# Residual row loads on SyncE, and the softmax's second half one PV step earlier, in a two-layer attention and token-MLP kernel

## The chip, the cores and the metric

The kernel runs on one core of one Trainium2 chip. The metric is the device time of one execution in microseconds. Of the kernel before, five runs gave a median of 1326.21 us (1325.14 to 1326.72). A difference of under some 0.2% between two kernels can hardly be told from none.

A core has five engines, each of which works through its own instructions in order: TensorE (matmuls into PSUM banks; PE in the profile, with PEld for the weight loads), VectorE (DVE), ScalarE (ACT), GpSimd (POOL) and SyncE (SP), which only issues DMA transfers. DMA transfers are issued by SyncE, GpSimd and ScalarE and carried out by 16 DMA engines. In the profile, q1 holds the transfers of SyncE and q0 those of GpSimd.

## The reference

Two kinds of residual layer alternate, twice: `x = x + A(layernorm(x))`, then `x = x + B(layernorm(x))`. x is 2048 rows by 1024 columns in bf16.

```
def A(x):   # 32 heads of 32; each row sees itself and 7 rows before it, 2 rows apart
    q, k, v = split(x @ wqkv)
    idx = pos[:, None] - 2 * arange(8)
    logits = einsum("bhsd,bhswd->bhsw", q, k[idx]) * 32 ** -0.5   # -1e9 where idx < 0
    o = einsum("bhsw,bhswd->bhsd", softmax(logits), v[idx])
    return o @ wo

def B(x):   # an MLP over the row axis S, not over the columns
    u = gelu(einsum("bsd,sf->bdf", layernorm(x), w1) + b1)        # F = 3584
    return (einsum("bdf,fs->bds", u, w2) + b2).transpose
```

## The kernel before

Since the window steps by two, even and odd rows never meet in A. They are two classes, c = 0 and 1, of 1024 rows each, held as 8 tiles of 128 rows. One layer of the program (`li` = 0 or 1, called layer 1 and layer 2 below) is one A and one B.

**Attention** of a class goes through two groups of 512 columns, so a layer has four groups, n = 0 to 3 (0 and 1 are class 0). For each group, `qk` (L431 to L444) multiplies q by eight shifted copies of k on VectorE (L439) and lets TensorE sum over each head with a selection matrix (L444). The softmax over the eight offsets is in two halves. `softmax_front` (L448) copies the logits, masks them, subtracts the maximum (last L455) and takes exp on ScalarE (L456). `softmax_back` (L458) sums, takes the reciprocal and multiplies (L461 to L465), stores the probabilities Pb in DRAM (L468) and calls `spread` (L474), which loads them back with each head's row repeated over 32 partitions, in two loads of 1 MB, one for each half hf of the rows (L482). These tiles, pb, come from a pool of two buffers. `pv` (L484) is a generator of steps: for one group, half of its columns and one hf, it yields two steps, dq = 0 and 1. A step is two products (L500), two additions (L504) and one more that writes oT (L506), all on VectorE; its scratch tile shares two buffers with qk's.

`stream` (L509) sets the order: in the second half of group n, qk, `softmax_front(n)`, the projections of the next columns, the hf = 0 steps of `pv(n - 1, ...)`, `softmax_back(n)`, the hf = 1 steps. After the last group come the eight PV steps of group 3 with no qk ahead of them; in layer `li` = 1, `ahead` does the same for group 1 in the middle.

**Output projection.** `out_proj` (L590) multiplies oT by wo, adds the residual row tile xr (VectorE, L625 or L628), stores the sum xn in DRAM on GpSimd (L630) and normalises it for B. `fetch` (L605) loads xr two tiles ahead; the load is issued by GpSimd (L608).

**MLP.** `gemm1` (L645) applies w1; `gemm2_tile` (L670) applies w2 to one row tile: it loads the residual rows xs, issued by GpSimd (L672), runs 56 matmuls, 28 for each half of the columns into a PSUM bank of its own, evicts them with bias and residual (VectorE, L686) into xo, stores xo on GpSimd (L692), normalises it into hb and has SyncE transpose hb into hT for the next attention (L233).

**Buffers and queues.** The row tiles xr, xn, xs, xo, hb, the scratch tiles junk and tmp share one pool, x2, of four slots, handed out as they come free. The weight tiles wo, w1, w2 and some of wv share a pool of five, and are loaded on SyncE, as are the wq tiles and the transposes. So SyncE's queue carries weights and transposes; GpSimd's carries row loads, row stores, Pb and pb.

**Order of the work.** The program's order is made in two stages. `weave` counts estimated times of TensorE and VectorE from the yields and places units of "filler" (the second class's GEMM2, projections ahead of time, the output projection of class 0, partial sums of GEMM1) between the attention's units. Then the framework's scheduler goes through all instructions by priority (their place in the program), with a model of times and of free slots, and fixes the order on every engine and queue; each instruction then waits on semaphores for what it needs. A lower instruction can so move ahead of a higher one that isn't ready in the model.

Of the kernel before, what the change touches and what calls it, by code (L numbers as in the profile page):

```python
# [15 lines left out]
P = 128  # L16
# [10 lines left out]
def kernel(  # L27
# [13 lines left out]
    nc = tc.nc  # L41
# [139 lines left out]
    def rows(t):  # L181
        return t.rearrange("(i m) d -> i m d", m=P)
# [166 lines left out]
    class Attn:  # L349
# [131 lines left out]
                src = bass.AP(base.tensor, base.offset, [(4 * SB * W * TB, CH), (0, P // CH), (1, 4 * W * TB)])  # L481
                nc.gpsimd.dma_start(out=pb[:].rearrange("p b u t -> p (b u t)"), in_=src)  # L482

        def pv(self, n, half, hf):  # L484


            c = n // NCQ
            for dq in (2 * half, 2 * half + 1):
                dt = (n % NCQ) * DQ + dq
                if hf == 0 and c and dt < 2 * DIL:  # L490
                    self.oT[c][dt] = v_t[dt // 2][:, dt % 2, PADK + 8:PADK + 8 + SC]
                elif hf == 0:
                    self.oT[c][dt] = otp.tile([P, SC], BF16, name="oT", tag="oT")[:]
                waits = [("pb", n, hf)] + ([] if c else [("ready", 2, dt)])
                yield "dve", 4.7, waits, [("free", 2, dt % 2), "oT"] if hf else [], 0.0, 0.0
                pb = self.pbs[(n, hf)]
                pr = tpl.tile([P, 4, W, TB], BF16, name="pr", tag="T")
                for par in range(2):
                    u = slice(4 * par, 4 * par + 4)
                    nc.vector.tensor_tensor(out=pr[:, :, u, :], in0=pb[:, :, u, :],  # L500
                                            in1=window(self.v_of(c, dt), par, 2 + hf * HT, [(TB, 4), (2, 4), (1, TB)]),
                                            op=ALU.mult)
                for wd in (4, 2):
                    nc.vector.tensor_tensor(out=pr[:, :, 0:wd, :], in0=pr[:, :, 0:wd, :], in1=pr[:, :, wd:2 * wd, :],  # L504
                                            op=ALU.add)
                nc.vector.tensor_tensor(out=self.oT[c][dt][:, hf * HT:(hf + 1) * HT].rearrange("p (b t) -> p b t", t=TB),  # L506
                                        in0=pr[:, :, 0, :], in1=pr[:, :, 1, :], op=ALU.add)

        def stream(self, lead):  # L509


            last = DIL * NCQ - 1
            PC = KD // 2

            def where(n, half):
                return n // NCQ, (n % NCQ) * (DQ // 2) + half

            def qk_proj(n, half):
                c, pair = where(n, half)
                if c == 1 and pair == 0:  # L520
                    yield "drain", "second"
                yield from self.proj_pair(c, pair, (1, 0))

            def v_proj(n, half):
                if n < NCQ:
                    yield from self.proj_pair(*where(n, half), (2,))

            def opened_by(n):
                if n == NCQ - 1:
                    yield "open", "out0"  # L530
                    yield "open", "partials"
                elif n == NCQ:
                    yield "open", "late"

            def ahead():
                c, pair = where(NCQ - 1, 1)
                for half in range(self.early):
                    if half:
                        for dt in (2 * pair, 2 * pair + 1):
                            for hf in range(2):  # L540
                                yield from self.proj(c, 2, dt, hf)
                    for hf in range(2):
                        yield from self.pv(NCQ - 1, half, hf)
                if self.early == 2:
                    yield from opened_by(NCQ - 1)

            yield from lead if lead is not None else qk_proj(0, 0)
            yield "open", "second"
            if lead is not None:
                yield "drain", "second"  # L550
            yield "open", "v_ahead"
            for n in range(last + 1):
                done = self.early if n == NCQ else 0
                for half in range(2):
                    nx = (n + half, 1 - half)
                    turn = nx == (NCQ, 0) and self.li > 0
                    yield from self.qk(n, 2 * half)
                    yield from self.qk(n, 2 * half + 1)
                    if half:
                        yield from self.softmax_front()  # L560
                    if lead is not None and nx == (0, 1):
                        for u in ((0, 2, 1), (0, 3, 0), (0, 3, 1),):
                            yield from self.proj(0, *u)
                    elif nx[0] <= last and not turn:
                        yield from qk_proj(*nx)
                    if n - 1 == NCQ and half == 0:
                        yield "drain", "v_ahead"
                    pv = n > 0 and half >= done
                    if pv:
                        yield from self.pv(n - 1, half, 0)  # L570
                    if half:
                        yield from self.softmax_back(n)
                    if pv:
                        yield from self.pv(n - 1, half, 1)
                        if half:
                            yield from opened_by(n - 1)
                    if n > 0 and half == 0 and done < 2:
                        yield from v_proj(n - 1, 1)
                    if half:
                        yield from v_proj(n, 0)  # L580
                    if nx == (NCQ, 0):
                        yield from ahead()
                    if turn:
                        yield from qk_proj(*nx)
            yield "drain", "out0"
            for half in range(2):
                for hf in range(2):
                    yield from self.pv(last, half, hf)

    def out_proj(at_, c, res, dst, h2, on_act):  # L590

        if not on_act:
            yield "pe", 0.0, ["oT"], [], 0.0
        dst_v = rows(dst)
        wo_t = [[None, None] for _ in range(NDC)]
        for n in range(NDC):
            for hf in range(2):
                wt = wb("wo", [P, KD // 2, 512])
                nc.sync.dma_start(out=wt[:], in_=wo_v[hf, :, :, n * 512:(n + 1) * 512])
                wo_t[n][hf] = wt  # L600
        for hf in range(2):
            h2[c][hf] = hx(f"h2{c}{hf}", [P, NT // 2, D])
        xrs = []

        def fetch():  # L605
            if len(xrs) < NT:
                xrs.append(x2("xr"))
                nc.gpsimd.dma_start(out=xrs[-1][:], in_=res[len(xrs) - 1])  # L608

        fetch()  # L610
        fetch()
        for i in range(NT):
            if not on_act:
                yield "pe", 3.5, ["oT"], [], 3.6
            xr = xrs[i]
            xn = x2("xn")
            s1 = st("s1", [P, NDC]) if on_act else None
            for n in range(NDC):
                ps = bank()
                xs_ = slice(n * 512, (n + 1) * 512)  # L620
                for kt in range(KD):
                    nc.tensor.matmul(ps[:], lhsT=at_.oT[c][kt][:, i * P:(i + 1) * P], rhs=wo_t[n][kt // 4][:, kt % 4, :],  # L622
                                     start=(kt == 0), stop=(kt == KD - 1))
                if on_act:
                    nc.vector.scalar_tensor_tensor(out=xn[:, xs_], in0=ps[:], scalar=1.0, in1=xr[:, xs_], op0=ALU.mult,  # L625
                                                   op1=ALU.add, accum_out=s1[:, n:n + 1])
                else:
                    nc.vector.tensor_tensor(out=xn[:, xs_], in0=ps[:], in1=xr[:, xs_], op=ALU.add)  # L628
            fetch()
            nc.gpsimd.dma_start(out=dst_v[i], in_=xn[:])  # L630
            h = h2[c][i // 4][:, i % 4, :]
            if on_act:
                nm, rs = stats_act(xn[:], 1.0 + EPS, eps2, h, s1)
                norm_act(h, xn[:], nm, rs)
                yield 3.5, 0.0
            else:
                mean, rs = stats_dve(xn[:], 1.0 + EPS, eps2)
                norm_dve(h, xn[:], mean, rs)
# [30 lines left out]

    def gemm2_tile(c, i, w2t, src, dst, hT, on_act=False, end=False):  # L670
        xs = x2("xs")
        nc.gpsimd.dma_start(out=xs[:], in_=src[c][i * P:(i + 1) * P, :])  # L672
        xo = x2("xo")
        halves = [slice(n * 512, (n + 1) * 512) for n in range(NDC)]
        groups = [halves[:1], [slice(512, 768)], [slice(768, 1024)]] if end else [halves]
# [105 lines left out]
    for li in range(2):  # L781
# [3 lines left out]
        res = [xin_v[c] for c in range(DIL)] if first else [rows(xb[c]) for c in range(DIL)]  # L785
# [89 lines left out]
```

## Time and profile before

| | |
|---|---|
| median of 5 runs | 1326.21 us (1325.14 to 1326.72) |
| the profiled execution's own time | 1326.21 us |
| its span, first to last instruction | 1324.4 us |
| mean granted TensorE clock | 0.987 |
| VectorE, ScalarE, GpSimd busy | 52%, 33%, 7% |
| DMA | 173 MB, 131 GB/s on average |
| median us to landing: xs (256 KB), xr (256 KB, from the input), pb (1 MB) | 3.9, 3.9, 11.0 |
| median us to landing: w2 tile (448 KB), w1 tile (512 KB) on SyncE | 3.8, 4.4 |

The profile is one execution on the chip. A group of instructions is named by engine, line and tiles: `xo<-ps,b_sb,xs` writes xo and reads ps, b_sb and xs. Waits are listed as who waited for whom, with total time, number and longest. The stages of the span, with the busy time of TensorE and VectorE in each:

| stretch, us | work | TensorE busy | VectorE busy |
|---|---|---|---|
| 0 to 200 | layer 1: class 0 prepared, its attention | 186.8 of 200 | 167.5 |
| 200 to 341 | class 1's attention, output projections, partial GEMM1 | 133.0 of 141 | 122.4 |
| 341 to 478 | GEMM1 | 136.8 of 137 | 30.4 |
| 478 to 574 | GEMM2 of class 0 | 96.0 of 96 | 24.1 |
| 574 to 781 | GEMM2 of class 1, woven with layer 2's attention of class 0 | 198.6 of 207 | 136.2 |
| 781 to 972 | class 1's attention, output projections, partial GEMM1 | 182.4 of 191 | 146.3 |
| 972 to 1128 | GEMM1 | 156.0 of 156 | 33.2 |
| 1128 to 1324 | GEMM2 of both classes | 193.3 of 196 | 23.6 |

TensorE idles almost only in the stretches with attention.

### The profile page before, as it was taken

The page shows a single profiled execution, that of the slowest core. Times are in us where ns is not written, and L with a number is a line of the kernel's source. Part 1 is how long each engine was busy: PE and PEld are TensorE (multiplying, and loading weights), DVE is VectorE, ACT ScalarE, POOL GpSimd, SP SyncE. Part 2 cuts the span into 40 slices and gives each one's busy share as a digit, 9 for nine tenths or more (in the row PEclk, how much of TensorE's full clock was granted, in tenths as well). Part 3 has the DMA queues.
Part 4 walks back from the last instruction along what each step waited for, and adds up shares of the span by engine and source line. Part 5 has one row for each costly group of instructions (what it writes and reads, how often), then busy time and mean ns, then how long its engine had stood idle before and what let it go on. Part 6 is the DMA issues. An engine that isn't in the chain of part 4 may idle for free.

```text
span 1324.4 us, 15430 instructions
## 1 busy us (share of the span) xinstructions
PE 1282.9 (97%) x6284; PEld 576.8 (44%) x6284; DVE 683.5 (52%) x861; ACT 439.7 (33%) x740; POOL 95.5 (7%) x230
## 2 busy tenths in 40 slices
PE   9998998999999999999997999999899999999999
PEld 4343443443444444444443444444344444444444
DVE  6779997989202322234796734878950033111111
ACT  6844445731213420024434425475122234000000
POOL 3000001101000000000001010011010000000000
PEclk9998999998999999999998999999899999999999
DMA  9652535562522248864658762438162232334432
GB/s 259 156 119 65 134 98 147 162 159 86 144 84 76 76 137 215 217 171 117 159 151 231 195 177 64 96 113 230 49 198 64 74 86 72 118 96 137 118 117 61
DMA packets 239448, 173.00 MB, mean 131 GB/s; under 512 B 32208, under 2 KB 227152, under 8 KB 237328
## 3 DMA queue, kind: packets, MB, share of 16 engines
q1 hardware_dynamic: 224432, 116.67, 32.7%
q0 software_dynamic: 14368, 54.29, 14.9%
q8 instruction: 49, 0.80, 0.3%
q10 hardware_dynamic: 576, 1.05, 0.2%
q14 instruction: 23, 0.19, 0.1%
HBM read 146.81 MB, written 18.87 MB: 125 GB/s over the span
## 4 chain that ended last, share of the span: by engine, by line
PE 65%; DVE 12%; DMA 6%; issue 1%; ACT 1%; DVEq 0%; POOL 0%; POOLq 0%
PE ps L681 24%; PE ps L655 22%; PE ps L409 11%; PE ps L622 6%; DVE pr L500 5%; DVE pr L504 4%; DMA xs<-xa 2%; DMA xa<-xn 1%; DMA pb<-pd 1%; PE sc L444 1%; DMA wq<-in_A_wqkv_dram 1%; DMA pd<-Pb 1%; DVE xo L686 1%; DVE T L439 1%; DMA hT<-hb 0%
## 5 line engine op out<-in xcount | busy, mean ns | idle before, releaser
L681 PE MATMUL ps<-g,w 128*128 128x512 bf16 (+1 forms) x1820 | 391.1, 377 | 7.5 <-DVE xo L686 7.5
L655 PE MATMUL ps<-h,w 128*128 128x512 bf16 x1792 | 388.2, 379 | 1.9 <-ACT h L230 1.3
L681 PEld LDWEIGHTS <-w 128*128 128x128 bf16 x1820 | 177.8, 98 | 218.9 <-issue 12.2
L655 PEld LDWEIGHTS <-w 128*128 128x128 bf16 x1792 | 175.3, 98 | 214.1 <-issue 3.3
L409 PE MATMUL ps<-hT,wq 128*128 128x512 bf16 (+1 forms) x1112 | 243.7, 376 | 2.1 <-DMA hT<-hb 1.1
L686 DVE SCALAR_TENSOR_TENSOR xo<-ps,b_sb,xs 128x512 bf16<-128x512 f32 (+1 forms) x65 | 45.6, 738 | 254.9 <-PE ps L681 230.6
L666 DVE TENSOR_TENSOR tmp<-ps,g 128x512 f32<-128x512 f32 x80 | 55.3, 692 | 227.4 <-PE ps L655 227.4
L439 DVE TENSOR_TENSOR T<-q,k 128x4096 bf16<-128x4096 bf16 x60 | 136.0, 2287 | 65.7 <-ACT q L413 54.1
L409 PEld LDWEIGHTS <-wq 128*128 128x128 bf16 x1112 | 108.6, 100 | 132.5 <-issue 12.7
L504 DVE TENSOR_TENSOR pr<-pr 128x2048 bf16<-128x2048 bf16 (+1 forms) x128 | 119.3, 948 | 0.1
L622 PE MATMUL ps<-wo,oT 128*128 128x512 bf16 x384 | 93.8, 386 | 13.0 <-DVE oT L506 9.3
L409 PE MATMUL ps<-hT,wv 128*128 128x512 bf16 x448 | 104.6, 388 | 0.0
L416 ACT CAST k<-ps 128x1024 bf16<-128x1024 f32 x60 | 60.9, 1016 | 78.0 <-PE ps L409 78.0
L500 DVE TENSOR_TENSOR pr<-pb,v 128x2048 bf16<-128x2048 bf16 x64 | 75.9, 1215 | 17.9 <-DMA pb<-pd 14.3
L667 ACT ACTIVATE g<-tmp,b_sb 128x512 bf16<-128x512 f32 x80 | 57.7, 721 | 82.1 <-DVE tmp L666 82.1
L500 DVE TENSOR_TENSOR pr<-pb,g 128x2048 bf16<-128x2048 bf16 x64 | 76.3, 1216 | 10.9 <-DMA pb<-pd 10.9
L409 PEld LDWEIGHTS <-wv 128*128 128x128 bf16 x448 | 49.2, 113 | 53.0 <-issue 10.7
L661 ACT CAST g<-ps 128x512 bf16<-128x512 f32 x80 | 45.5, 591 | 68.7 <-PE ps L655 68.6
L192 ACT ACTIVATE ln<-mv,eps 128x1 f32<-128x1 f32 x37 | 10.9, 295 | 164.2 <-DVE mv L201 156.8
L622 PEld LDWEIGHTS <-oT 128*128 128x128 bf16 x384 | 37.3, 99 | 63.4 <-issue 11.7
L413 ACT CAST q<-ps 128x512 bf16<-128x512 f32 x60 | 35.0, 585 | 52.2 <-PE ps L409 52.2
L444 PE MATMUL sc<-T,sel 128*32 128x512 bf16 x512 | 39.3, 394 | 11.5 <-DVE T L439 11.4
(94 smaller groups left out, 632.8 us busy)
## 6 DMA issues: line engine op xcount, KB each, us to landing
w<-in_B_w_dram SPq DMA_DIRECT2D x96, 448.0 KB, 3.8
w<-in_B_w_dram SPq DMA_DIRECT2D x56, 512.0 KB, 4.4
wq<-in_A_wqkv_dram SPq DMA_DIRECT2D x38, 512.0 KB, 4.2
pb<-pd POOLq DMA_DIRECT2D x16, 1024.0 KB, 11.0
wo<-in_A_wo_dram SPq DMA_DIRECT2D x16, 512.0 KB, 4.4
xa<-xn POOLq DMA_DIRECT2D x32, 256.0 KB, 3.5
xs<-xa POOLq DMA_DIRECT2D x32, 256.0 KB, 3.9
wv<-in_A_wqkv_dram SPq DMA_DIRECT2D x14, 512.0 KB, 6.7
```

What stands on the lines that cost most here:

```text
L409: nc.tensor.matmul(ps[:, lo:hi], lhsT=cols, rhs=self.hT[c][hf][:, kt, lo:hi], start=(kt == 0), stop=(kt == KD - 1))
L416: nc.scalar.copy(out=window(buf, 0, PADK + hf * HT, [(KW + 1, 2), (1, HT)]), in_=ps[:].unsqueeze(1).to_broadcast([P, 2, HT]))
L439: nc.vector.tensor_tensor(out=T[:], in0=q.unsqueeze(1).to_broadcast([P, 4, SC]), in1=window(k, par, 2, [(2, 4), (1, SC)]), op=ALU.mult)
L444: nc.tensor.matmul(self.sc[32 * gr:32 * gr + 32, par], lhsT=sel[:, sb * DQ + dq, :], rhs=T[:, :, b * TB:(b + 1) * TB], start=(dq == 0 and ...
L500: nc.vector.tensor_tensor(out=pr[:, :, u, :], in0=pb[:, :, u, :], in1=window(self.v_of(c, dt), par, 2 + hf * HT, [(TB, 4), (2, 4), (1, TB) ...
L504: nc.vector.tensor_tensor(out=pr[:, :, 0:wd, :], in0=pr[:, :, 0:wd, :], in1=pr[:, :, wd:2 * wd, :], op=ALU.add)
L622: nc.tensor.matmul(ps[:], lhsT=at_.oT[c][kt][:, i * P:(i + 1) * P], rhs=wo_t[n][kt // 4][:, kt % 4, :], start=(kt == 0), stop=(kt == KD - 1))
L655: nc.tensor.matmul(ps[:], lhsT=wt[c][:, i, fl * P:(fl + 1) * P], rhs=h2[c][i // 4][:, i % 4, dc * 512:(dc + 1) * 512], start=(k == 0), sto ...
L666: nc.vector.tensor_tensor(out=tmp[:], in0=ps[:], in1=gs, op=ALU.add)
L667: nc.scalar.activation(out=gs, in_=tmp[:], func=ACT.Gelu_apprx_tanh, bias=b1_sb[:, ft:ft + 1])
L681: nc.tensor.matmul(ps[:, 0:xc.stop - xc.start], lhsT=w2t[n][:, ft % HF, c::DIL], rhs=g[ft // GF][:, ft % GF, xc], start=(ft == 0), stop=(f ...
L686: nc.vector.scalar_tensor_tensor(out=xo[:, xc], in0=ps[:, 0:xc.stop - xc.start], scalar=b2_sb[:, i, c:c + 1], in1=xs[:, xc], op0=ALU.add, ...
```

## The change

The change has two parts; the second and third points below belong together.

- The loads of the residual rows, xr in `out_proj` and xs in `gemm2_tile`, are issued by SyncE and not by GpSimd: 32 loads of each kind, 256 KB apiece. The stores of the rows stay on GpSimd.
- `pv` takes an argument `dqs`, the steps to make; by default both, as before.
- In `stream`, of the two hf = 0 steps of `pv(n - 1, ...)`, only dq = 0 stands ahead of `softmax_back(n)`; dq = 1 comes after it. In the half without a `softmax_back` the two steps follow each other as before. The oT tiles of the columns are handed out in the same order.

```diff
-        def pv(self, n, half, hf):
+        def pv(self, n, half, hf, dqs=(0, 1)):
 
 
             c = n // NCQ
-            for dq in (2 * half, 2 * half + 1):
+            for dq in (2 * half + x for x in dqs):
                 dt = (n % NCQ) * DQ + dq
@@ stream
                     pv = n > 0 and half >= done
                     if pv:
-                        yield from self.pv(n - 1, half, 0)
+                        yield from self.pv(n - 1, half, 0, (0,))
                     if half:
                         yield from self.softmax_back(n)
                     if pv:
+                        yield from self.pv(n - 1, half, 0, (1,))
                         yield from self.pv(n - 1, half, 1)
@@ out_proj
         def fetch():
             if len(xrs) < NT:
                 xrs.append(x2("xr"))
-                nc.gpsimd.dma_start(out=xrs[-1][:], in_=res[len(xrs) - 1])
+                nc.sync.dma_start(out=xrs[-1][:], in_=res[len(xrs) - 1])
@@ gemm2_tile
         xs = x2("xs")
-        nc.gpsimd.dma_start(out=xs[:], in_=src[c][i * P:(i + 1) * P, :])
+        nc.sync.dma_start(out=xs[:], in_=src[c][i * P:(i + 1) * P, :])
```

## The prediction

> **What bounds the kernel now.** I read the page first, then TensorE's waits, then the order of time around each of its stalls on every queue that the change touches.
>
> ```profile
> span 1324.4 us, 15430 instructions
> PE 1282.9 (97%) x6284; PEld 576.8 (44%) x6284; DVE 683.5 (52%) x861; ACT 439.7 (33%) x740; POOL 95.5 (7%) x230
> ```
>
> TensorE is the bound. Nothing here takes matmuls away, so the gain can only come from its 1324.4 - 1282.9 = 41.5 us of idle time and from matmuls that ran at half clock after a stall. The waits of TensorE over the run, longest first in total (us, times, longest):
>
> ```profile
> PE sc L444 <- DVE T L439: 11.4, 3, 5.3
> PE ps L622 <- DVE oT L506: 9.3, 3, 6.1
> PE ps L681 <- DVE xo L686: 7.5, 1, 7.5
> PE ps L622 <- DMA wo<-in_A_wo_dram: 3.7, 2, 3.1
> ```
>
> The third is one stall, at 709.7 to 717.2, in the stretch where GEMM2 of class 1 is woven with the second layer's attention. The GpSimd and SyncE queues there (start, duration, instruction, idle time before it and its releaser):
>
> ```profile
> 696.74 0.65 POOL L468 DMA_DIRECT2D pd<-Pb  x1 [16.49 <-DVE pr L500]
> 702.33 1.06 POOL L482 DMA_DIRECT2D pb<-pd  x2 [4.94 <-issue]
> 703.85 0.59 POOL L692 DMA_DIRECT2D xb<-xo  x1 [0.46 <-DVE xo L686]
> 704.65 0.55 POOL L672 DMA_DIRECT2D xs<-xa  x1 [0.22 <-ACT t L216]
> ...
> 696.59 8.14 SPq L709 DMA_DIRECT2D w<-in_B_w_dram  x3
> 708.34 1.42 SPq L233 DMA_TRANSPOSE hT<-hb  x1
> ```
>
> The row load xs is issued behind 2 MB of pb and a store. The transfers of 700 to 718 (KB each, us from issue to landing):
>
> ```profile
> wq<-in_A_wqkv_dram SPq DMA_DIRECT2D x2, 512.0 KB, 9.1
> w<-in_B_w_dram SPq DMA_DIRECT2D x1, 448.0 KB, 12.9
> xs<-xa POOLq DMA_DIRECT2D x1, 256.0 KB, 11.6
> ```
>
> An xs takes 3.9 us in the median of the page, 11.6 here; but the SyncE queue is as slow at this moment. VectorE reaches xo at 716.40, as xs lands; before, it had waited for pb until 710.42 and then worked 1.2 us. So 716.4 - 711.6 = 4.8 us of the 7.5 belong to xs, the rest to pb.
>
> The longest wait for oT (6.1 us, 938.1 to 944.2) is the end of layer 2's attention. VectorE before it:
>
> ```profile
> 892.62 1.21 DVE L455 TENSOR_TENSOR L<-L,m 128x1024 f32<-128x1024 f32 x1
> ...
> 899.92 0.67 DVE L461 TENSOR_TENSOR m<-L 128x512 f32<-128x512 f32 x1
> ...
> 904.56 1.20 DVE L465 TENSOR_TENSOR Pb<-L,m 128x1024 bf16<-128x1024 f32 x1
> ...
> 918.90 3.50 DVE L500 TENSOR_TENSOR pr<-pb,g 128x2048 bf16<-128x2048 bf16 x3 [5.46 <-DMA pb<-pd]
> ```
>
> ScalarE's exp ends at 895.0, but the second half of the softmax (L461 to L465) starts 4.9 us later, behind products of the PV step that stands ahead of it. Then come the store of Pb, the load of pb (8.2 us) and an idle VectorE.
>
> [...] in 704 to 717 the DMA share is 1.04, and all queues are slow. [...] xs of 256 KB lands in 3.9 us from GpSimd, w of 448 KB in 3.8 us from SyncE. So the move helps only by the place in a queue. [...] undisturbed, 140 matmuls take 30.38 us (0.217 each); after the stall at 717.2, 69 take 16.43 us where 15.0 are due (1.5 lost); after 944.2, 12 take 4.84 us where 2.6 are due (2.2 lost).
>
> **The change, part by part.**
>
> *64 loads leave GpSimd for SyncE.* 32 xs and 32 xr at 0.54 us are 34.8 us off GpSimd, worth nothing in themselves: it is busy for 7%. On SyncE they cost 64 issues of 0.37 us or more (one weight load's row), some 24 to 35 us, spread over a queue that mostly waits for TensorE to free weight buffers. Bytes are the same.
>
> *Place of xs at 704.65.* I take it that the planner puts xs on SyncE where it found it schedulable before, at about the first write of hb (702.6), since every xs of the steady GEMM2 also comes after its predecessor's rows are evicted. The third of the three w loads waits for matmuls that end at 704.2. If xs goes ahead of it, it shares the engines with pb from 702.7 on and lands by about 709, ahead of pb. Gain: the 4.8 us, and about half of the 1.5 us at half clock. If it goes behind that w, which landed at 717.3, the gain is 0, or a loss of 1 to 2 us. I take the first: VectorE's part ends before TensorE's. What is late next is the chain to the last hT of this stage (TensorE waits 1.1 us for it at 781.8): it hangs on VectorE, which moves with xo, and on the last xs (8.5 us to land, issued at 765.7 when a transpose frees its slot). Behind 1 MB of wv on SyncE it lands no later. Stage: -5.5 us, ends -8 and +2.
>
> *Second half of the softmax one PV step sooner.* No instruction is added. pb's first buffer is now still read by PV's dq = 1 when its load is traced, so that load gets a wait for those products; they end before Pb's store lands (4.5 us after its issue), so it costs nothing as long as the store takes over about 3 us. Behind this load on GpSimd stand the second pb, which waits for the hf = 1 products anyway, and the xa or xb stores. VectorE already fills the gaps of the dependent softmax chain with PV operations, so that a step of 4.7 us moves less than 4.7 us. In four of the six places L461 starts only 2.3 to 3.4 us after L455's end, with exp needing about 1.3 of it: there Pb gains 0.5 to 1.1 us. At 893.8 it starts 6.1 us after; exp ends at 895.0, and the chain's own 3.3 us with 3.2 us of fill between would end at 901.6 instead of 905.7: 4.1 at most. I take 3, and 1 more[...]. TensorE's 6.1 us become some 2, and 1 us of the half clock's 2.2 goes with it. Layer 2's end: -5, ends -8 and 0. Layer 1's end has stalls of 1.5 and 1.7 us at 301 to 305 and, afterwards, 21 matmuls in 7.36 us where 4.6 are due; Pb gains up to 1.1 there: -1, ends -6 and 0. For the others: pb is loaded under the next QK products (four of 2.3 us each), so 0; at 200 to 215, where a store behind pb holds VectorE for 5.0 us, -0.5.
>
> *Added waits on SyncE.* xr and xs wait for one of four slots, and weights, transposes and wo stand behind them. In steady GEMM2 a w is issued when the fourth step ahead of its use ends: 4 steps of 3.02 us are 12.1 us of lead, less 3.8 us of landing: 8.3 us of slack. A wait for a transpose's landing (3.4 to 4.5 us) is covered; the two early xr at 35 and 42 stand between transposes whose own waits are on ScalarE and come later. wo has no slack (3.1 us stall at 196)[...]. I book +2 for all.
>
> Sum: -5.5 - 5 - 1 - 0.5 + 2 = -10. Planned order moves a few PE instructions with it, for which I give back 1.5: the span 1324.4 becomes 1316, and with the 1.8 us that lie around it (the profiled execution took 1326.21, exactly the median) 1317.7.
>
> **The rivals.**
> 1. *Only one half pays* (xs lands late, or L461 stays put): -3 to -7, about 1321. For it: the two gains hang on different choices of the planner, and DMA is full where xs is.
> 2. *No difference*: xs falls behind w in its ring, and the PV operations fill in as before: 1326. For it: four of six softmaxes are already interleaved; against it: the 4.9 us at 895.
> 3. *SyncE is held up*, the case of the other sign. An xs that waits for the landing of a transpose stands in front of w. Place: 574 to 781, where GpSimd waited 24.7 us in 4 waits for hT before an xs, up to 9.2 us. It decides once such a hold passes the slack of 8.3 us; a transpose took 9.8 us to land in the full stretch, and w 12.9. Price: two or three stalls of 2 to 3 us, each with 1.5 us of half clock, and the gain of xs is gone: about +6, 1332. Against it: POOL's waits include the time before the transpose was issued, which SyncE need not wait again.
> That the change doesn't do its work: the loads move for certain; the softmax may not (rival 2).
>
> **The numbers.** Both halves pay: 42%, 1310 to 1322. One half: 20%, 1318 to 1323. No difference: 16%. SyncE held up: 22%, 1329 to 1338. Faster by over 0.2% (2.7 us, about what a measurement can tell from no change): 62%; within it 16%; slower 22%. The range for 8 in 10 leaves out some 6% below (all upper ends together) and 14% above, of rival 3 the longer part: 1309 to 1331. The likeliest case alone: 1310 to 1322.
>
> **What would show it.** Right: xs near 703 on SyncE and landed by 710; the 7.5 us stall below 3; L461 within 3 us of L455's end at layer 2's last softmax; the wait for oT near 2 us; slightly fewer half-clock stretches. Wrong: TensorE waiting for w or wq, which it hardly does now (0.2 us for wq); xs behind w; the stall at 717 merely moved to the last hT at 781. A new order in which VectorE delays QK products would show as longer waits for T (11.4 us now).

## The result, and the profile after

The kernel after takes 1322.8 us in the median of 31 runs (1318.3 to 1326.7), the kernel before 1325.9 us in 52 runs beside them (1323.2 to 1330.1): a ratio of 0.9974 (95% interval 0.9967 to 0.9981). That is 3 us faster, where 8.5 us were forecast. The time lies inside the predicted range and just outside the likeliest case's own range, 1310 to 1322.

The profiled execution of after took 1319.62 us, with a span of 1317.9; a second execution had a span of 1324.6. The part of the page on spans and busy times:

```profile
span 1317.9 us, 15470 instructions
PE 1281.1 (97%) x6284; PEld 576.3 (44%) x6284; DVE 682.5 (52%) x861; ACT 439.5 (33%) x740; POOL 61.1 (5%) x166
```

The 64 loads are off GpSimd: its busy time fell by 95.5 - 61.1 = 34.4 us, where 34.8 were worked out. TensorE's waits (us in total, times, longest):

```profile
PE ps L623 <- DVE oT L506: 8.3, 3, 3.9
PE sc L444 <- DVE T L439: 7.1, 4, 5.2
PE ps L409 <- DMA wv<-in_A_wqkv_dram: 6.2, 1, 6.2
PE ps L623 <- DMA wo<-in_A_wo_dram: 2.9, 2, 2.3
PE ps L682 <- DVE xo L687: 2.5, 1, 2.5
```

The wait for xo fell from 7.5 to 2.5 us, the longest for oT from 6.1 to 3.9, those for T from 11.4 to 7.1 in total. The third line is new: one wait of 6.2 us for a wv tile. The waits of before list none for wv.

**The new wait.** SyncE, GpSimd and TensorE around it, in the timeline of after (start, duration, instruction, idle time before it and its releaser):

```profile
132.47 1.02 POOL L482 DMA_DIRECT2D pb<-pd  x2 [4.06 <-issue]
132.78 0.37 SPq L387 DMA_DIRECT2D wv<-in_A_wqkv_dram  x1
146.91 1.90 PE L409 MATMUL ps<-hT,wv 128*128 128x512 bf16 x4 [6.16 <-DMA wv<-in_A_wqkv_dram]
```

The same place in before:

```profile
134.33 0.37 SPq L387 DMA_DIRECT2D wv<-in_A_wqkv_dram  x1
135.17 1.02 POOL L482 DMA_DIRECT2D pb<-pd  x2 [4.08 <-DMA pd<-Pb]
```

The DMA issues of this stretch (count, KB each, median us from issue to landing), of after:

```profile
pb<-pd POOLq DMA_DIRECT2D x2, 1024.0 KB, 10.6
wv<-in_A_wqkv_dram SPq DMA_DIRECT2D x1, 512.0 KB, 14.1
```

and of before:

```profile
pb<-pd POOLq DMA_DIRECT2D x2, 1024.0 KB, 12.0
wv<-in_A_wqkv_dram SPq DMA_DIRECT2D x1, 512.0 KB, 3.6
```

The order of two queues has turned round. Before, wv went out 0.84 us ahead of the 2 MB of pb and landed in 3.6 us. After, it goes out 0.31 us behind them and lands in 14.1 us. SyncE issues wv when TensorE's matmuls (L409) free its buffer, which has not changed (between 120 and 150 us SyncE waits 33.9 us for them at L387 in both); Pb is what comes sooner (8.56 us from L455 to L465, 9.69 before).

Why 0.3 us behind pb cost wv 10 us can be read from the packets in which the profile records the transfers. Between 136 and 143 us of after both queues had work (packets and MB in all, then those of each queue, with its share of the 16 DMA engines):

```profile
DMA packets 413, 1.65 MB, mean 235 GB/s; under 512 B 16, under 2 KB 241, under 8 KB 241
q0 software_dynamic: 187, 1.40, 87.2%
q1 hardware_dynamic: 225, 0.23, 15.6%
```

The two queues moved about as many packets, 187 and 225. But those of pb (q0) hold 8 KB (172 of the 413 are of that size or more, and make up its 1.40 MB), and those of wv and of the wo behind it (q1) 1 KB (0.23 MB in 225). At about even numbers of packets SyncE's queue got a seventh of the bytes, and wv landed only when pb's second load did: at 132.8 + 14.1 = 146.9 us, the other at 133.0 + 13.4 = 146.4.

**The forecast gains.** In the stretch of the second stall, timeline of after:

```profile
701.06 0.50 SPq L673 DMA_DIRECT2D xs<-xa  x1
705.34 0.37 SPq L710 DMA_DIRECT2D w<-in_B_w_dram  x1
713.16 15.05 PE L682 MATMUL ps<-g,w 128*128 128x512 bf16 x69 [2.46 <-DVE xo L687]
```

Here xs goes out ahead of the last w, TensorE waits 2.46 us instead of 7.49, and the 69 matmuls after it take 15.05 us instead of 16.43. At layer 2's end (VectorE, timeline of after):

```profile
886.40 1.21 DVE L455 TENSOR_TENSOR L<-L,m 128x1024 f32<-128x1024 f32 x1
889.08 0.67 DVE L461 TENSOR_TENSOR m<-L 128x512 f32<-128x512 f32 x1
895.04 1.20 DVE L465 TENSOR_TENSOR Pb<-L,m 128x1024 bf16<-128x1024 f32 x1
909.59 1.23 DVE L500 TENSOR_TENSOR pr<-pb,g 128x2048 bf16<-128x2048 bf16 x1 [2.84 <-DMA pb<-pd]
```

From L455 to L461 pass 2.7 us instead of 7.3, from L455 to Pb 8.6 instead of 11.9, and the wait for pb is 2.8 us instead of 5.5.

**Where the 6.5 us between the two spans come from.** Marks that both timelines have, and how far after stands behind before (+) or ahead (-) at each, with what the stretch added:

| mark on TensorE | before | after | difference | this stretch |
|---|---|---|---|---|
| end of the wait for wo, near 200 | 199.40 | 205.69 | +6.3 | +6.3 |
| long block of GEMM1 that follows (L655) | 253.69 | 255.83 | +2.1 | -4.2 |
| end of the wait for xo | 717.21 | 713.16 | -4.1 | -6.2, of which 5.0 that wait |
| layer 2's last QK block (L444) | 885.63 | 879.41 | -6.2 | -2.2 |
| GEMM1 of both classes begins | 972.32 | 963.99 | -8.3 | -2.1 |
| end | 1324.4 | 1317.9 | -6.5 | +1.8 |

The first row is the loss. It is about 9 us, of which 2.4 us are masked: the profiled execution of before happened to be late there (it has a stretch of 3.4 us at half clock, a granted clock of 0.50, near 40 us that no other profile has; with the loads alone, below, this mark is at 196.98). The last row is a small loss that the forecast doesn't have either. The two spans differ by twice as much as the medians do, since the profiled execution of after is 3.2 us faster than its median.

### The profile page after: what moved, and what is told of

Same layout as the page of the kernel before. It is cut to its first block, busy times and chain, and to the rows that moved or that the text cites. A ratio compares the mean times of both kernels' runs of the same rounds, so it can differ in the third digit from the quotient of the medians.

```text
span 1317.9 us, 15470 instructions
## 1 busy us (share of the span) xinstructions
PE 1281.1 (97%) x6284; PEld 576.3 (44%) x6284; DVE 682.5 (52%) x861; ACT 439.5 (33%) x740; POOL 61.1 (5%) x166
## 5 line engine op out<-in xcount | busy, mean ns | idle before, releaser
L409 PE MATMUL ps<-hT,wq 128*128 128x512 bf16 (+1 forms) x1112 | 243.8, 376 | 0.7 <-ACT t L273 0.4
L409 PEld LDWEIGHTS <-wq 128*128 128x128 bf16 x1112 | 108.8, 100 | 131.3 <-issue 13.8
L409 PE MATMUL ps<-hT,wv 128*128 128x512 bf16 x448 | 104.1, 386 | 6.2 <-DMA wv<-in_A_wqkv_dram 6.2
L409 PEld LDWEIGHTS <-wv 128*128 128x128 bf16 x448 | 48.8, 112 | 58.6 <-issue 9.3
L192 ACT ACTIVATE ln<-mv,eps 128x1 f32<-128x1 f32 x37 | 10.9, 295 | 155.8 <-DVE mv L201 148.6
L416 ACT CAST g<-ps 128x1024 bf16<-128x1024 f32 x36 | 36.5, 1017 | 47.9 <-PE ps L409 47.9
```

The lines of the kernel that those rows point to most:

```text
L409: nc.tensor.matmul(ps[:, lo:hi], lhsT=cols, rhs=self.hT[c][hf][:, kt, lo:hi], start=(kt == 0), stop=(kt == KD - 1))
L416: nc.scalar.copy(out=window(buf, 0, PADK + hf * HT, [(KW + 1, 2), (1, HT)]), in_=ps[:].unsqueeze(1).to_broadcast([P, 2, HT]))
```

## The experiments

Each experiment was timed beside the kernel before, and ratios are to that. They were timed in three groups, in which the kernel before took 1326.1 us (after once more, the loads, the softmax, layer 2's groups), 1325.1 us (xs, xr, the one group, everywhere but there) and 1326.4 us (the others); between groups the ratios compare better than the times.

**The kernel after once more**, for a second profile, without any edit.

> The changed kernel itself, for a second look beside its parts. Theory (collision): in layer 1's second group Pb is now ready 2.7 us sooner, so the 2 MB load of pb is issued just ahead of the wv load (132.5 against 132.8 us; before, 135.2 against 134.3) and wv lands in 14 us instead of 4, which costs TensorE about 6 us and half clock after it. Being a race of a few tenths of a us, it needn't fall out the same way in each execution, which would explain why this kernel's times are spread (1318.3 to 1326.7 us). Median 1321 to 1324 us. Rival (SyncE's queue): wv is late because of the row loads on its own queue. The same time.

1321.53 us (1317.95 to 1326.64, 19 runs), ratio 0.9969 (0.9959 to 0.9980). The wait for wv is there again (issued 0.37 us behind pb, landing in 14.7 us), though this execution is 6.7 us longer than the other. What differs is the clock. The lines below give, for 700 to 730 us, the busy time of each engine; the third figure from the end is the granted clock. In after:

```profile
700.00:730.00 30.00, 27.54 (x129) 13.03 (x128) 22.94 (x29) 13.90 (x28) 2.18 (x4) 1.00 1.09 258
```

and in the second execution:

```profile
700.00:730.00 30.00, 25.38 (x106) 11.50 (x107) 21.05 (x26) 13.89 (x28) 2.17 (x4) 0.89 1.03 236
```

Here the wait for xo was 2.46 us in the first and 4.34 us in the second, and only the second has half clock after it. Over the whole span, windows of 2 us show 27.6 us at half clock in the first and 37.4 us in the second, always in pieces of 3.4 or 6.8 us. At a granted clock of 0.50 TensorE made 6 matmuls in 2 us (936 to 938 of after), at 1.00 it made 11 (942 to 944), so half of the 9.8 us of difference were lost, 4.9 of the 6.7 us. So the wait for wv came in both, and the spread of the times is largely how many stalls were followed by half clock: of the executions on record with the result, those with a mean granted clock of 0.986 took 1325.7 to 1326.7 us and those with 0.990 or more 1318.3 to 1320.3 us.

**One half of the change at a time.** The loads alone, on the kernel before:

```diff
-                nc.gpsimd.dma_start(out=xrs[-1][:], in_=res[len(xrs) - 1])
+                nc.sync.dma_start(out=xrs[-1][:], in_=res[len(xrs) - 1])
-        nc.gpsimd.dma_start(out=xs[:], in_=src[c][i * P:(i + 1) * P, :])
+        nc.sync.dma_start(out=xs[:], in_=src[c][i * P:(i + 1) * P, :])
```

> Row loads on SyncE, PV and softmax in the old order. Collision theory: no wait for wv, the stall for xo near 713 is 2 to 3 us instead of 7.5, the wait for oT at layer 2's end is about 6 us as before: 1319 to 1321 us. Rival: the wait for wv near 147 us, of about 6 us, is there without the new softmax order: 1323 to 1326 us.

The softmax alone: the kernel after with these two lines turned back.

> New order of softmax and PV, row loads on GpSimd as before. Collision theory: the wait for wv of about 6 us is there, the 7.5 us stall for xo stays, the wait for oT at layer 2's end is 2 to 4 us instead of 6: the two cancel, 1325 to 1328 us. Rival: no wait for wv; 1322 to 1324 us.

The loads alone: 1318.87 us, 0.9939 (0.9926 to 0.9953). The softmax alone: 1334.46 us, 1.0059 (1.0046 to 1.0071). The loads gain some 7 us, with a wait for xo of 4.8 us where I had expected 2 to 3. The softmax's new order, which the forecast credited with 6.5 us of gain, loses 8 us alone and 4 us on top of the loads. For it alone I had expected 1325 to 1328 us, with a wait for oT at layer 2's end of 2 to 4 us. That wait is 5.9 us: Pb comes as early as in after (8.64 us from L455), but the row loads still go out on GpSimd ahead of pb and beside it, and the first pb takes 10.6 us to land, not 7.6. So by these profiles the gain at layer 2's end hangs on the loads too. The wait for wv belongs to the softmax: with the loads alone wv is issued at 131.91, pb at 132.72, and wv lands in 3.6 us; with the softmax alone, 131.44 and 131.19, in 14.5 us. That also refutes that wv is late because SyncE's queue is longer.

**Which load.** The kernel before with only one of the two lines moved:

```diff
-        nc.gpsimd.dma_start(out=xs[:], in_=src[c][i * P:(i + 1) * P, :])
+        nc.sync.dma_start(out=xs[:], in_=src[c][i * P:(i + 1) * P, :])
```

> The kernel before with only the xs loads of GEMM2 on SyncE. If the loads' gain is the place of one xs at 704 us, as I predicted: stall for xo 2 to 5 us instead of 7.5, no wait for the last hT, 1319 to 1321 us, most of what both loads give (1318.9). If the xr loads matter as much: 1322 or more.

```diff
-                nc.gpsimd.dma_start(out=xrs[-1][:], in_=res[len(xrs) - 1])
+                nc.sync.dma_start(out=xrs[-1][:], in_=res[len(xrs) - 1])
```

> The kernel before with only the xr loads of the output projection on SyncE. If the xs loads carry the gain: 1325 to 1327 us, with the 7.5 us stall for xo as before. If xr matters: the stall at 211 us (4.4 us before, 3.1 with both loads moved) shrinks and the time is 1323 or less.

xs alone: 1320.61 us, 0.9964 (0.9952 to 0.9976), with a wait for xo of 1.85 us. xr alone: 1322.6 us, 0.9979 (0.9971 to 0.9988), with that wait at 6.43 us. So the xs step was right in place and size (4.5 us by the medians, 4.8 by the ratio; 4.8 forecast), though the wait for the last hT, which I had expected to go, is still 1.3 us. xr gains 2.8 us by the ratio, to which the forecast gave nothing. I had expected it at the stall for T near 211 us, but that is longer with xr alone (5.2 us, 4.4 before). Its profile is 2 us ahead of before's by 200 us, but so is that with xs alone, where xr is untouched, so that lead is before's own slow start. It is level with before at 254 us (253.64 and 253.69) and 2.0 us ahead where GEMM1 ends (475.63 and 477.64); 1.7 us of this are a half-clock stretch of 3.4 us instead of 6.8 near 304. Whether the median's gain is the same these profiles don't show.

**The new softmax order in some groups only**, always with the loads on SyncE. The form of the edit, with the groups as the condition (here layer 2's three groups, `self.li` = 1):

```diff
-                        yield from self.pv(n - 1, half, 0, (0,))
+                        yield from self.pv(n - 1, half, 0, (0,) if self.li else (0, 1))
                     if half:
                         yield from self.softmax_back(n)
                     if pv:
-                        yield from self.pv(n - 1, half, 0, (1,))
+                        if self.li:
+                            yield from self.pv(n - 1, half, 0, (1,))
```

> Both parts, but the new softmax order in layer 2 alone. Collision theory: wv lands in about 4 us, no wait for it, and everything gained in layer 2 stays: 1315 to 1318 us, with a narrower spread than the changed kernel's. Rival: the wait for wv stays; 1321 to 1324 us, as the changed kernel.

Only in layer 1's second group, `(self.li, n) == (0, 1)`:

> Row loads on SyncE; the new softmax order in one place only, layer 1's second group (n = 1). Collision theory: this place alone brings the wait for wv of 6 to 7 us with half clock after it, and nothing is gained elsewhere: 1325 to 1328 us, against 1318.9 for the loads alone. Rival (the loss in layer 1 comes from the later groups, or from the new order as a whole): no wait for wv, within 2 us of 1318.9.

Everywhere but there, `(self.li, n) != (0, 1)`:

> The changed kernel with the old softmax order in that one place (layer 1, n = 1) and the new one in the five others. Collision theory: no wait for wv, all other gains stay: 1314 to 1317 us, like the new order in layer 2 alone (1314.8). Rival: still 1320 or more.

Layer 2: 1314.83 us, 0.9913 (0.9899 to 0.9926). The one group: 1328.33 us, 1.0025 (1.0015 to 1.0035). Everywhere else: 1311.79 us, 0.9904 (0.9891 to 0.9917). One group of six costs 9.5 us on top of the loads (11.4 by the ratios), and the kernel after without it is 11 us faster (9.3 by the ratios), 2 us below what I had expected. Timeline of the kernel with the new order in that group alone:

```profile
132.31 1.02 POOL L482 DMA_DIRECT2D pb<-pd  x2 [4.04 <-issue]
132.64 0.37 SPq L387 DMA_DIRECT2D wv<-in_A_wqkv_dram  x1
147.28 1.90 PE L409 MATMUL ps<-hT,wv 128*128 128x512 bf16 x4 [6.67 <-DMA wv<-in_A_wqkv_dram]
```

and of the kernel with the old order there alone:

```profile
131.90 0.37 SPq L387 DMA_DIRECT2D wv<-in_A_wqkv_dram  x1
132.64 1.02 POOL L482 DMA_DIRECT2D pb<-pd  x2 [3.98 <-issue]
```

**The collision itself.** These kernels change the order of VectorE's work in that group together with the issue of pb. To part them, the kernel after keeps its order, and pb alone is made to wait until wv has landed, by a copy of one element:

```diff
                 self.pbs[(n, hf)] = pb
+                if (self.li, n) == (0, 1):
+                    self.weights(0, 2, DQ)
+                    nc.gpsimd.tensor_copy(out=pb[0:1, 0, 0, 0:1], in_=self.weights(1, 2, DQ)[1][0:1, 0, 0:1])
```

> The kernel after, with one thing more: in layer 1's group n = 1 each of the two pb loads is held by a one-element copy on GpSimd that reads the late wv tile, so they are issued after wv has landed. The softmax keeps its new order everywhere, Pb is as early as in the kernel after, and the order on TensorE, VectorE, ScalarE and SyncE is unchanged. Theory (the collision of pb with wv is the cost, not the order of the operations): wv lands in about 4 us, TensorE's wait of 6 us for it and the half clock after it are gone, and the time is that of split_not_first, 1312 us (1309 to 1316); pb is issued near 137 and lands near 146, as in the kernel before (145.7). Rival (the new order in this place costs by itself, for instance by keeping VectorE from the QK products): 1322 us (1318 to 1326), as the kernel after, and a stall near 141 to 150 of another name.

1313.93 us (1310.59 to 1315.48), 0.9907 (0.9892 to 0.9921). Its timeline there:

```profile
131.43 0.37 SPq L387 DMA_DIRECT2D wv<-in_A_wqkv_dram  x1
134.99 2.37 POOL L482 COPY pb<-wv 1x1 bf16<-1x1 bf16 x2 [7.94 <-DMA wv<-in_A_wqkv_dram]
137.54 1.03 POOL L485 DMA_DIRECT2D pb<-pd  x2 [0.18 <-POOL pb L482]
138.35 1.92 PE L409 MATMUL ps<-hT,wv 128*128 128x512 bf16 x8
```

In this kernel wv lands in 3.4 us and TensorE doesn't wait for it. pb is issued 5 us later than in after, and VectorE waits 3 us longer for pb over the run (25.1 us, 22.2 in after). Holding 2 MB back by 5 us makes the kernel 9 us faster: the transfers' order is the cost, and the order on VectorE is not.

**The sizes of single groups**, each on top of the loads. Only layer 2's last group, `(self.li, n) == (1, last)`:

> The loads on SyncE, and the new softmax order only in layer 2's last group. Theory (the forecast's term for layer 2's end was too large, for the stall for oT shrinks by only about 2 us): -2 against the kernel with the loads alone, 1316 to 1318 us; L461 within 3.5 us of L455's start plus its 1.2, pb's wait on VectorE near 2.8 us, TensorE's wait for oT near 3.9. The forecast's own value: -5, 1313 to 1315, with a wait for oT near 2. Rival (nothing of it reaches the end): 1319.

Only layer 1's third group, `(self.li, n) == (0, 2)`:

> The loads on SyncE, and the new softmax order only in layer 1's third group (n = 2). Theory: the stall for T near 213 (3.1 us with the loads alone, 4.4 before) goes, and with it some half clock: -3, 1315 to 1317 us. The forecast's value was -0.5, 1318 to 1319, with a stall of over 2.5 us there. Rival (the stall moves to the load of wo or to oT after 290): 1319, with a longer wait there.

Only layer 2's second group, `(self.li, n) == (1, 1)`:

> The loads on SyncE, and the new softmax order only in layer 2's second group (n = 1), at 695 to 720 us, where pb and xs share the DMA engines. Theory: what the order brings to layer 2 beyond its end (about -2 of the -4.0 between loads_only and split_layer2) is here, since an earlier pb lets VectorE reach the row xo sooner: 1316 to 1318 us, the wait for xo near 2.6 us instead of 4.8. The forecast gave this place 0: 1319, and the wait for xo 4 to 5 us. Rival (pb ahead of xs makes xs late): a wait for xo of over 5 us, 1320 or more.

*Layer 2's last group*: 1318.52 us, 0.9938 (0.9919 to 0.9957), no different from the loads alone. The rival that gave it nothing was right, although L461, pb's wait (2.88 us) and oT's (3.92 us) are all as my theory had them. TensorE in the timeline with the loads alone:

```profile
900.44 29.08 PE L655 MATMUL ps<-h,w 128*128 128x512 bf16 x132 [0.68 <-ACT h L230]
...
936.97 0.61 PE L622 MATMUL ps<-wo,oT 128*128 128x512 bf16 x1 [5.71 <-DVE oT L506]
```

and with the new order in this group:

```profile
902.46 27.36 PE L657 MATMUL ps<-h,w 128*128 128x512 bf16 x126 [1.76 <-ACT h L230]
...
935.24 0.61 PE L624 MATMUL ps<-wo,oT 128*128 128x512 bf16 x1 [3.92 <-DVE oT L506]
```

From the last QK block to GEMM1 of both classes pass 84.4 us instead of 86.8, a gain of 2.4. But the last block of partial GEMM1 ahead of the stall is 27.36 us long instead of 29.08: eight matmuls of 0.217 us, 1.7 us, have moved behind it. (Of the loads alone some matmul records are missing, so that its counts are short; in the full records of before and after the block has 134 and 126.) From GEMM1 of both classes to the end pass 353.9 us instead of 352.1 (963.82 to 1317.7; 965.57 to 1317.7). All kernels with the new order in this group have 353.8 to 353.9 there, all others 352.1 to 352.2. The stall shrank largely because work that used to stand ahead of it was taken out.

*Layer 1's third group*: 1309.65 us (1307.01 to 1313.16, 4 runs), 0.9887 (0.9869 to 0.9905), beyond my theory's 1315 to 1317 and the fastest of all. From the end of the wait for wo to the long block of GEMM1 pass 48.5 us instead of 53.9 with the loads alone, 5.4 us. Timeline of the kernel before this one, which has the old order in layer 1 too, as the loads alone have:

```profile
197.44 1.02 PE L624 MATMUL ps<-wo,oT 128*128 128x512 bf16 x4 [3.17 <-DMA wo<-in_A_wo_dram]
199.49 0.58 POOL L632 DMA_DIRECT2D xa<-xn  x1 [2.30 <-DVE xn L627]
203.33 0.34 SPq L610 DMA_DIRECT2D xr<-in_A_x_dram  x1
211.36 0.69 DVE L627 SCALAR_TENSOR_TENSOR xn<-ps,xr 128x512 bf16<-128x512 f32 x1 [5.86 <-DMA xa<-xn]
214.32 1.04 PE L444 MATMUL sc<-T,sel 128*32 128x512 bf16 x8 [5.27 <-DVE T L439]
```

and of the kernel with the new order in this group:

```profile
196.16 1.02 PE L624 MATMUL ps<-wo,oT 128*128 128x512 bf16 x4 [2.37 <-DMA wo<-in_A_wo_dram]
198.21 0.59 POOL L632 DMA_DIRECT2D xa<-xn  x1 [2.31 <-DVE xn L627]
204.15 0.68 DVE L627 SCALAR_TENSOR_TENSOR xn<-ps,xr 128x512 bf16<-128x512 f32 x1
209.25 1.42 SPq L610 DMA_DIRECT2D xr<-in_A_x_dram  x2
```

In the first, the row load xr is issued at 203.33 and the third row's xn has to wait for a slot. It starts at 211.36, as the first store xa lands (199.49 + 11.7 = 211.2, behind pb on GpSimd's queue), and T for QK stands behind it on VectorE. In the second, xn runs at 204.15 and the load of xr waits instead, until that store has landed (198.21 + 10.9 = 209.1). xr, xn and the others share four slots: the new order gave the free slot to the user that TensorE waits for. That is read from these times; no run hands the slots out by hand. With the softmax alone, where xr is still on GpSimd, the stall stays (3.0 us, and 54.8 us for the stretch), so by these profiles this gain needs both halves of the change.

The rest of its gain lies in waits that shrank downstream and in clock. Windows of 290 to 330 us, layer 1's end, in this kernel:

```profile
290.00:330.00 40.00, 36.76 (x170) 16.34 (x169) 38.36 (x65) 5.64 (x20) 4.39 (x8) 1.00 0.43 138
```

and in the kernel with the new order everywhere but in the second group:

```profile
290.00:330.00 40.00, 35.22 (x149) 15.38 (x151) 37.24 (x64) 5.42 (x19) 4.37 (x8) 0.91 0.47 147
```

The stalls for oT here are 1.56 and 1.68 us with full clock after them, against 2.77 and 1.68 us with 6.8 us at half clock. The first of the two goes with the order of layer 1's last group: it is 2.46 to 2.84 us in the five profiles with the new order there and 0.97 to 1.92 us in the nine with the old one. So in that group the new order costs about a microsecond, though Pb comes 1.1 us sooner.

*Layer 2's second group*: 1319.54 us, 0.9955 (0.9941 to 0.9968), nothing gained. Pb is written 8.56 us after L455, exactly as with the loads alone, so the new order moves nothing here. Yet the wait for xo is 6.39 us against 4.77: VectorE waits for pb until 708.61 in one and 708.85 in the other. In that case everything ahead of it ran 1.9 us earlier and the gain stayed in this wait. The kernels with xs on SyncE have waits from 1.85 to 6.4 us here; the order of this group doesn't decide between them, as both my theory and the rival had it. The wait goes with the time that pb's first load takes to land: 12.8 us here, 12.3 with the loads alone, 8.9 with the new order in all of layer 2, where the wait is 2.65 us. What sets that time was not settled.

**The version to keep**: the loads on SyncE and the new order in layer 1's third group alone, 1309.65 us, is faster than before (0.9887) and than after. The new order everywhere but in the second group (0.9904) can't be told from it: the intervals overlap. The groups' gains don't add up: layer 2's three groups together gain 4 us on the loads, its second and its last alone nothing, and in its second and third Pb comes no sooner at all (8.56 and 4.85 us after L455, in before as in after). The profile of the three together has full clock after its stalls for xo and oT, where that of the loads alone has 10.2 us of half clock; that alone is worth 5.1 us. A combination of the third group with others wasn't tried.

## Why the prediction was right or wrong

The direction was right, and the size wrong: -3 us instead of -8.5. The forecast's steps:

- *"For the others: pb is loaded under the next QK products (four of 2.3 us each), so 0"*: this is the step that failed. I asked who waits for pb, found nobody, and booked an earlier Pb at nothing. I didn't ask what the earlier 2 MB would run into. In layer 1's second group Pb came 1.1 us sooner, as the forecast itself had it (0.5 to 1.1), and wv was only 0.84 us ahead. So pb overtook this load of 512 KB by 0.3 us, and its time to land went from 3.6 to 14 us: +9 us (by the edits 8.9 to 11.4, by the profile 6.2 us of wait and 3.4 us lost in 6.8 us at half clock). I had taken it that two queues at work share the DMA engines evenly, which no trace had shown. Counted in packets the two did so between 136 and 143 us of after, with 187 and 225; counted in bytes, as I had meant it, they didn't, with 1.40 and 0.23 MB.
- *Place of xs*, stage -5.5: right. xs went to SyncE ahead of the last w, at 701.1, and the stage from xo's stall to the last QK block gained 5.0 + 2.2 = 7.2 us, with the wait for the last hT (1.1 us) gone too. It landed at 701.1 + 10.7 = 711.8 and not by 709, half a microsecond behind pb and not ahead of it, but VectorE, which had waited for pb until 711.2, came to xo only at 712.4. So what was left of the stall was pb's, as the forecast had it.
- *Layer 2's end*, -5: the second step that failed, in size. The chain on VectorE was right (Pb 3.3 us sooner; 3 taken), the net was about 0. The extra microsecond for the landing of the first pb was my estimate and didn't come: its two loads go out 2.4 us apart, but the first still took 7.6 us (8.3 before), and pb came 3.1 us sooner in all. The stall kept 3.9 us instead of 2, with a granted clock of 0.50 after it, from 933.80 on. And 1.8 us of the 2.1 gained came back later, as eight filler matmuls had moved out of the stall's cover.
- *Layer 1's end*, -1: nothing, and a loss but for the clock. The two stalls went from 3.2 to 4.4 us in all; that the half clock fell from 6.8 to 3.4 us is luck, since of the four other profiles with the new order there three have 6.8 us.
- *The stretch 200 to 215*, -0.5: -4.2 us in the profile of after, -5.4 in that of the group alone. The forecast saw the store behind pb that holds VectorE, and not that the new order could hand the slot round it.
- *Added waits on SyncE*, +2: none found. TensorE waits for neither w nor wq, and the longest wait for wo went from 3.1 to 2.3 us.
- *Rival 3*, SyncE held up: refuted, the loads alone are 7 us faster. *Rival 2*, no difference: wrong, though for layer 2's second group it describes what happened. *Rival 1*, only one half pays, came nearest with 1321 us: the loads pay and the softmax takes back half, but for a reason that it doesn't name. The forecast's list of what would show it wrong has TensorE waiting for w or wq, and not for wv.

That the time lies within the predicted range is in part luck. The case given the best chance, that both halves pay, is not what happened, and the missing +9 us was hidden by gains larger than forecast at xs and at 200 to 215: with pb held back the kernel gains 12 us, more than the 8.5 forecast.

The forecast booked half clock after each long stall. In the profiles it comes after stalls too, at a granted clock of 0.50 and in pieces of 3.4 or 6.8 us; 2.4 us of wait for xo were enough in the kernel with the new order in layer 1's third group alone, where the 69 matmuls after it take 16.74 us instead of the 15.05 of after. But whether it comes is not told by the stall's length: 2.5 us at xo brought none, 4.3 us did, and 3.87 us at oT brought none in the kernel with layer 2's groups alone, where 3.88 us did in after. What decides can be worked out from the traces. Within each profile the granted clock changes only at points that lie whole multiples of 3.41 us apart. The lines below cut the span at these points; after the piece's length stands TensorE's busy time, and the third figure from the end is the clock. In after the stall for oT lies mostly in one piece:

```profile
930.38:933.80 3.42, 0.94 (x5) 0.20 (x3) 3.42 (x5) 0.05 (x1) 0.00 (x0) 1.00 0.50 176
933.80:937.21 3.41, 2.01 (x5) 0.73 (x6) 3.41 (x6) 0.00 (x0) 0.00 (x0) 0.50 0.00 0
```

With the new order in layer 2's groups alone it is shared between two:

```profile
925.38:928.80 3.42, 1.51 (x8) 0.49 (x5) 3.42 (x4) 0.59 (x1) 0.00 (x0) 1.00 0.61 216
928.80:932.21 3.41, 1.44 (x7) 0.70 (x8) 3.41 (x5) 0.00 (x0) 0.00 (x0) 1.00 0.00 0
932.21:935.62 3.41, 3.36 (x16) 1.39 (x15) 3.41 (x5) 0.00 (x0) 0.00 (x0) 1.00 0.00 0
```

TensorE was busy for 27% of the first piece, and half clock followed; 44% and 42% in the two others brought none. In the 14 profiles of this case, 75 of the 76 falls to half clock follow a piece with TensorE busy for 41% or less (the other is that of before near 40 us, 49%), and no piece of 41% or less was followed by full clock. As an estimate from these figures, a stall of 2.0 us (59% of 3.41) would bring half clock if it fell within one piece, one of 4.0 us wherever it fell, and between the two it would depend on where the points happen to lie.

## What to carry to other kernels

When an edit makes a large transfer start sooner, don't stop at who waits for it: list what every other queue issues in the next few microseconds, and check that none of it is needed soon. Look at the packets too: here a load in packets of 1 KB, beside one in packets of 8 KB, got a seventh of the bytes. A margin of 0.8 us between two queues is not an order, and where it matters, make the large transfer wait for the small one. And when a stall shrinks, count the work that stood ahead of it before and after, up to a mark well behind it: half of the gain may be work that was only moved.

## What was not expected of the hardware

- 512 KB issued on SyncE 0.25 to 0.37 us behind 2 MB on GpSimd landed in 14.1 to 14.7 us in all four profiles with that order; issued 0.84 us ahead, it landed in 3.6 us in before, and 0.74 us ahead in 3.8 us with the new order everywhere but in layer 1's second group.
- Between 136 and 143 us of after, where both queues had work, they moved about as many packets, 187 and 225, and these held 1.40 and 0.23 MB.
- Times of one and the same kernel spread over 8 us, and two profiled executions differ by 6.7. Some 5 us of that are half clock after stalls that came in both, one of them 2.46 us long in one and 4.34 us in the other.
- The granted clock changes at points 3.41 us apart, and it fell after a piece between them in which TensorE was busy for 41% or less, in 75 of 76 falls; a stall of 3.88 us was followed by half clock and one of 3.87 us was not.
